# FFT filter and gated feed-forward on one core: the second and third transform stage as three products of high and low parts

## The chip, the core and the metric

The kernel runs on one NeuronCore of a Trainium2 chip. The metric is the time of one execution on the device in microseconds (us). A profile of one execution shows each engine's instructions: TensorE (PE, with its weight loads as PEld), VectorE (DVE), ScalarE (ACT), GpSimd (POOL) and SyncE (SP), which issues nearly all transfers.

## What is computed

```python
X = np.fft.rfft(x, axis=1)                      # x: 8 x 3136 x 256, float32
y = np.fft.irfft(X * (filt_r + 1j * filt_i), n=3136, axis=1)
h = np.maximum(y @ w_in, 0.0)                   # 256 -> 1024
conv = sum(conv_w[k] * shift(h, k - 1) for k in range(3))   # along the sequence
out = (h * sigmoid(conv)) @ w_out               # 1024 -> 256
```

The Fourier transform of length 3136 = 112 x 28 is done in four stages of small matrix products, two forward (kinds 1 and 2) and two back (kinds 3 and 4), with the filter between kinds 2 and 3.

## The kernel before

**Transform.** A batch has 14 pairs of columns; each kind works pair by pair, so a batch has 14 operations of each kind. Kind 1 multiplies input columns by tables `s1` that differ from column to column and stores to `a_dram`. Kind 2 (`second`, L233) reads `a_dram` in another order and multiplies by one constant matrix `s2` (112 x 120); the last pair uses `s2s` for its second half. `filt` (L240) multiplies by the filter: three multiplications on DVE (L244 to L246) from the PSUM bank and one addition on POOL (L247) that makes `z`. Kind 3 multiplies `z` by tables `i1`, which differ from column to column because they hold the frequency factors, and stores to `b_dram`. Kind 4 (`fourth`, L250) uses one constant matrix `m2`. All four are plain float32 products. The result y is kept in SBUF as a high part (rounded to the product type `F32R`, on ACT) and a low part (the rest, on DVE or POOL).

**Feed-forward.** The sequence of all batches is cut into units of 510 tokens; each unit has 8 slices of the hidden width. `inner` makes a slice's h in a PSUM bank with `mm3` (L174): three products, high x high, high x low, low x high, here twice for the two halves of the inner dimension. `relu`, `centre`, `sigmoid` and `round_g` run on ACT, `tap` (twice) and `gate` on DVE, `rest_g` (the low part of g, L150) on POOL. `project` adds the slice to two PSUM banks with twelve products of 256 columns; after a unit's eighth slice `evacuate` (L518) copies the two banks on DVE and stores them.

**Order.** Batch 0 goes through all four kinds at first by itself (about 118 us, loads, conversion of the weights from double precision, and no feed-forward). Then comes the main loop of single steps m, one slice each: 48 steps per batch. Every engine works through its own instructions in the order in which the loop emits them. In step m the transforms of later batches are issued ahead of `inner(m)`, and behind it `project` of the slice six steps earlier. The bank of a transform is read in the next step: `from_bank` stores kinds 1 and 3 (ACT copies, L226), runs `filt` for kind 2, and copies kind 4, whose parts `to_y` makes. `evacuate` stands ahead of `from_bank`. POOL's order in a step is: addition of `filt`, `rest_g` of the slice four steps back, then the low part of y.

**Plan.** Lists `at2` and `at4` say in which of the 48 steps kinds 2 and 4 of a batch are done; kind 3 follows three steps behind kind 2, and kind 1 of the next batch goes to the steps with the least work. From batch 2 on `at2 = [2 + 9*q//5 for q in range(14)]`: steps 2, 3, 5, 7, 9, 11, 12, 14, 16, 18, 20, 21, 23, 25. Batch 1 has its own list, and the last batch's span has no kind 1. Evacuations fall on steps 6, 14, 22, 30, 38 and 46.

**Buffers.** Transforms share two PSUM banks (`ps_t`), `inner` has four, `project` two. Inputs (`tin`) have five buffers and are loaded up to five operations ahead by `want_in`; tables (`tab`) have four, filters two, `z` three, `ot` three.

Of the kernel before, what the change touches and what calls it, by code (L numbers as in the profile page):

```python
# [19 lines left out]
G = 28  # L20
# [16 lines left out]
def _dft_tables():  # L37
# [6 lines left out]

    n1, n2, c, a = np.arange(N1), np.arange(N2), np.arange(N2), np.arange(N1)
    s1 = np.zeros((N1, N2, 112))
    m2 = np.zeros((112, N1))
    i1 = np.zeros((2, 2, 28, G, N2, 4))
    for g in range(G):
        for s in range(2):  # L50
            if g == G - 1 and s == 1:
                s1[:, :, 2 * 28 + g] = 1.0
                s1[:, :, 3 * 28 + g] = ((-1.0) ** n1)[:, None]
                m2[2 * 28 + g] = 1.0 / S
                m2[3 * 28 + g] = (-1.0) ** a / S
                i1[0, s, 0, g, :, 2] = 1.0
                i1[1, s, 0, g, :, 2] = (-1.0) ** c
                for j in range(14):
                    if j:
                        w = np.conj(_w(j * c, N2))  # L60
                        i1[0, s, j, g, :, 2] = 2 * w.real
                        i1[1, s, j, g, :, 2] = -2 * w.imag
                    w = np.conj(_w((56 + 112 * j) * c, S))
                    i1[0, s, 14 + j, g, :, 3] = 2 * w.real
                    i1[1, s, 14 + j, g, :, 3] = -2 * w.imag
# [5 lines left out]
            w = np.conj(_w(k1 * a, N1))  # L71
            m2[2 * s * 28 + g] = 2 * w.real / S
            m2[(2 * s + 1) * 28 + g] = -2 * w.imag / S
            for j in range(28):
                k2, sg = (j, 1) if j < 14 else (41 - j, -1)
                w = np.conj(_w((k1 + 112 * k2) * c, S))
                i1[0, s, j, g, :, 2 * s] = w.real
                i1[1, s, j, g, :, 2 * s] = -sg * w.imag
                i1[0, s, j, g, :, 2 * s + 1] = w.imag
                i1[1, s, j, g, :, 2 * s + 1] = sg * w.real  # L80

# [22 lines left out]

    i1 = i1.reshape(2, 56, G, 112)
    i1 = np.concatenate([i1[0], np.zeros((8, G, 112)), i1[1]])
    return {"s1": s1, "s2": s2(False), "s2s": s2(True), "one": np.eye(128), "i1": i1, "m2": m2}

# [14 lines left out]
def tile_fft_filter_gated_ffn(  # L123
# [11 lines left out]
    one: bass.AP,  # L135
    i1: bass.AP,
    m2: bass.AP,
    out: bass.AP,
):
# [48 lines left out]
    wc = ctx.enter_context(tc.tile_pool(name="wc", bufs=1))  # L188
    m2_sb = wc.tile([112, N1], F32, name="m2_sb")
    s2_sb = wc.tile([112, 120], F32, name="s2_sb")  # L190
    s2s_sb = wc.tile([112, 120], F32, name="s2s_sb")
    one_sb = wc.tile([128, 128], F32, name="one_sb")
    cw = wc.tile([128, 3, NF], F32, name="cw")
# [55 lines left out]

    def fourth(ps, br, m=m2_sb):  # L250
# [11 lines left out]
    with (  # L262
# [4 lines left out]
        raws, ws, fts, tabs, rows, zs, pss = {}, {}, {}, {}, {}, {}, {}  # L267
        m2g = sc.tile([112, N1], F32, name="m2g", bufs=1)
        bt = sc.tile([128, KT, G, 112], F32, name="bt", bufs=1)
# [66 lines left out]
        with tc.tile_pool(name="sq", bufs=2) as sq:  # L336
            at = sq.tile([128, KT, N2, 112], F32, name="at", bufs=1)

            def table(kind, c):
                k, src, n = {"1": (112, s1, 7), "3": (120, i1, 3)}[kind]  # L340
                tabs[kind, c] = t = sq.tile([120, 4, 112], F32, name=f"tab{kind}", bufs=n)[0:k]
                nc.sync.dma_start(out=t, in_=src[:, 4 * c:4 * c + 4])
# [11 lines left out]
            for c in range(7):  # L354
                table("1", c)
                load_x(0, 2 * c)
                load_x(0, 2 * c + 1)
                if c == 0:
                    load_conv()
                if c in (1, 3):  # L360
                    load_weights(c // 2)
                if c == 4:
                    for dst, src in ((one_sb, one), (s2_sb, s2[:, 0:120]), (s2s_sb, s2s[:, 0:120])):
                        nc.sync.dma_start(out=dst, in_=src)
# [15 lines left out]
            for i in range(NP + 4):  # L380
# [26 lines left out]
        for q in range(NP + 1):  # L407
# [3 lines left out]
            if q:  # L411
                ps = bank()
                fourth(ps, rows.pop(("4", q - 1)), m2g)
                yh, yl = y_slices(0, pair(q - 1))
# [103 lines left out]
    def evacuate(u, f):  # L518
        if f < NF - 1:
            return  # L520
        for k in range(2):
# [3 lines left out]
            n = part[0][1]  # L525
            ot = wp.tile([128, 2, D], F32, name="ot", bufs=3)
            nc.vector.tensor_copy(ot[0:n, 0:len(part)].rearrange("p t d -> p (t d)"), pos[u][k][0:n, 0:len(part) * D])  # L527
# [26 lines left out]
    for t in range(1, B):  # L554
        w = NW * (t - 1)
        used = [0] * NW
        if t == 1:
            at1 = [q // 2 for q in range(NP - AHEAD)]
            at2, at4 = [8 + 3 * q // 2 for q in range(NP)], [33 + 11 * q // NP for q in range(NP)]
            for q, s in enumerate(at1):  # L560
                put(s, "1", 1, AHEAD + q)
                used[s] += 1
        else:
            at2, at4 = [2 + 9 * q // 5 for q in range(NP)], [32 + 12 * q // NP for q in range(NP)]
        for q in range(NP):
            for s, kind, cost in ((at2[q], "2", 3), (at2[q] + 3, "3", 1), (at4[q], "4", 1)):
                put(w + s, kind, t, q)
                used[s] += cost
        if t + 1 < B:
# [5 lines left out]
            for q, s in enumerate(sorted(spots)):  # L575
                put(w + s, "1", t + 1, q)
        tails[w + 29] = heads[w + 45] = next(u for u in range(NU) if joins(u) and place(u)[0] == t - 1)
# [3 lines left out]
    tables = [op for _, op in order if op[0] in "13"]  # L581
    filters = [op for _, op in order if op[0] == "2"]
# [8 lines left out]
    def want_in():  # L591
        while wanted["in"] < min(done["in"] + 5, len(inputs)) and ready(inputs[wanted["in"]]):
            op = inputs[wanted["in"]]
            wanted["in"] += 1
            got_in[op] = load_in(tp, *op, 5, "tin")
# [13 lines left out]
    def transform(op):  # L609
        kind, b, q = op  # L610
        banks[op] = ps = ps_t.tile([128, 512], F32, name="ps_t")
        if kind in "124":
            done["in"] += 1
            r = got_in.pop(op)
        if kind in "13":
            want_table(done["table"] + 3)
# [35 lines left out]
    with tc.manual_schedule(engines=COMPUTE | {mybir.EngineType.SP}):  # L652
# [4 lines left out]
        for m in range(NF * NU + PLAG + 1):  # L657
# [78 lines left out]
```

## Time and profile before

| | |
|---|---|
| time, median of 3 runs | 1586.02 us (1585.51 to 1588.09) |
| profiled execution | 1583.21 us, its span 1581.2 us |
| mean granted TensorE clock | 0.991 |
| TensorE / DVE / ACT / POOL busy | 1532.2 / 1180.3 / 1150.4 / 821.7 us |
| instructions in the span | 26837 |

The span is the time from the first to the last instruction of the profiled execution. In a timeline row stand the start, the time taken, the engine, the line, the operation, what it writes and reads, its shapes and count, and in square brackets how long the engine had been idle and what ended that. A float32 product counts as two instructions on TensorE, one of high and low parts (`F32R`) as one. A matmul's recorded time contains its way through the array, so rows of successive matmuls overlap; the distance of starts tells how long one occupies TensorE. A row of a stretch shows its limits, its length, then busy time and number of instructions of PE, PEld, DVE, ACT and POOL, and at the end the granted TensorE clock, the share of the transfer engines and GB/s.

### The profile page before, as it was taken

How to read it: one execution, taken by the hardware profiler on the slowest of the kernel's cores; microseconds unless marked ns; L12 is line 12 of the kernel's file. 1: busy time of each engine (PE TensorE's matmuls, PEld its weight loads, DVE VectorE, ACT ScalarE, POOL GpSimd, SP SyncE). 2: the span in 40 equal slices, each digit the busy share in tenths (PEclk: the TensorE clock that was granted, in tenths of full speed). 3: DMA queues.
4: the chain of work that ended last, by engine and by line, in shares of the span. 5: the costliest groups of instructions: out<-in, count | busy, mean ns of one | idle time of the engine just before them, and what ended most of it. 6: DMA issues, size and time to landing. Idle time of an engine off the chain costs nothing.

```text
span 1581.2 us, 26837 instructions
## 1 busy us (share of the span) xinstructions
PE 1532.2 (97%) x9384; PEld 1334.5 (84%) x9384; DVE 1180.3 (75%) x1810; ACT 1150.4 (73%) x1989; POOL 821.7 (52%) x703
## 2 busy tenths in 40 slices
PE   6879999999999999999999999999999999999999
PEld 5777789878898889988898878987899878989998
DVE  5856876677767877777766787777866887777776
ACT  3367668866687668866688667876678666888886
POOL 2623455544575455744556454754457445664444
PEclk9989999999999999999999999999999999999999
DMA  9808764366634674277543766246742553300000
GB/s 271 261 24 246 226 192 140 119 204 178 186 88 143 201 218 125 74 209 210 155 139 107 212 179 184 85 148 198 211 135 63 179 155 106 96 14 28 27 28 30
DMA packets 160592, 229.16 MB, mean 145 GB/s; under 512 B 16546, under 2 KB 109578, under 8 KB 160458
## 3 DMA queue, kind: packets, MB, share of 16 engines
q1 hardware_dynamic: 159497, 226.53, 48.0%
q8 instruction: 75, 1.23, 0.3%
q10 hardware_dynamic: 960, 0.92, 0.2%
q14 instruction: 60, 0.48, 0.1%
HBM read 156.74 MB, written 70.65 MB: 144 GB/s over the span
## 4 chain that ended last, share of the span: by engine, by line
PE 87%; DMA 3%; issue 3%; ACT 2%; DVE 2%; POOL 1%; SPq 0%; ACTq 0%; POOLq 0%; DVEq 0%
PE ps_h L175 11%; PE ps_h L176 11%; PE ps_h L177 11%; PE po L514 11%; PE po L515 11%; PE po L516 11%; PE ps_t L231 10%; PE ps_t L255 6%; PE ps_t L235 5%; DMA rows<-in_x 1%; DMA f<-in_filt 1%; POOL g L150 1%; DMA tab<-in_i 1%; ACT y L144 0%; ACT br L327 0%
## 5 line engine op out<-in xcount | busy, mean ns | idle before, releaser
L482 DVE SCALAR_TENSOR_TENSOR t<-ps_h,cw,t 128x510 f32<-128x510 f32 (+1 forms) x800 | 588.3, 736 | 308.2 <-ACT t L478 305.0
L150 POOL TENSOR_TENSOR g<-t,g 128x510 fp32r<-128x510 f32 (+1 forms) x400 | 505.8, 1273 | 219.5 <-ACT g L144 203.9
L514 PE MATMUL po<-wo,g 128*128 128x256 f32 (+1 forms) x1576 | 439.3, 279 | 0.2 <-DVE ot L527 0.2
L515 PE MATMUL po<-wo,g 128*128 128x256 f32 (+1 forms) x1576 | 438.3, 278 | 0.0
L516 PE MATMUL po<-wo,g 128*128 128x256 f32 (+1 forms) x1576 | 438.0, 278 | 0.0
L473 ACT ACTIVATE ps_h<-ps_h 128x512 f32<-128x512 f32 (+1 forms) x400 | 234.7, 587 | 242.2 <-PE ps_h L177 240.7
L478 ACT ACTIVATE t<-ps_h,cw 128x510 f32<-128x510 f32 (+1 forms) x400 | 272.7, 682 | 103.4 <-POOL g L150 71.3
L247 POOL TENSOR_TENSOR z<-z,v 120x512 f32<-120x512 f32 x112 | 148.0, 1322 | 383.4 <-DVE v L246 314.6
L175 PE MATMUL ps_h<-y,wi 128*128 128x512 f32 (+1 forms) x688 | 325.3, 473 | 0.0
L514 PEld LDWEIGHTS po<-wo,g 128*128 128x128 f32 (+1 forms) x1576 | 296.6, 188 | 17.8 <-ACT t L478 0.6
L515 PEld LDWEIGHTS po<-wo,g 128*128 128x128 f32 (+1 forms) x1576 | 296.2, 188 | 16.6
L516 PEld LDWEIGHTS po<-wo,g 128*128 128x128 f32 (+1 forms) x1576 | 296.4, 188 | 0.6 <-POOL g L150 0.5
L176 PE MATMUL ps_h<-y,wi 128*128 128x512 f32 (+1 forms) x688 | 269.4, 392 | 0.2 <-DVE y L147 0.2
L488 DVE TENSOR_TENSOR t<-ps_h,t 128x510 f32<-128x510 f32 (+1 forms) x400 | 268.4, 671 | 0.9 <-ACT t L485 0.8
L177 PE MATMUL ps_h<-y,wi 128*128 128x512 f32 (+1 forms) x688 | 269.0, 391 | 0.0
L485 ACT ACTIVATE t<-t 128x510 f32<-128x510 f32 (+1 forms) x400 | 245.2, 613 | 1.8 <-DVE t L482 1.7
L144 ACT ACTIVATE g<-t 128x510 fp32r<-128x510 f32 (+1 forms) x400 | 245.1, 613 | 0.2 <-DVE t L488 0.2
L150 POOL TENSOR_TENSOR y<-z,y 128x448 fp32r<-128x448 f32 x98 | 138.7, 1425 | 97.4 <-ACT y L144 92.9
L175 PEld LDWEIGHTS ps_h<-y,wi 128*128 128x128 f32 x688 | 129.9, 189 | 35.9 <-issue 16.6
L176 PEld LDWEIGHTS ps_h<-y,wi 128*128 128x128 f32 x688 | 130.4, 190 | 34.4 <-issue 16.7
L177 PEld LDWEIGHTS ps_h<-y,wi 128*128 128x128 f32 x688 | 129.6, 188 | 29.8
L226 ACT ACTIVATE st<-ps_t 112x512 f32<-112x512 f32 x192 | 113.2, 591 | 10.9 <-PE ps_t L231 10.9
(81 smaller groups left out, 1657.9 us busy)
## 6 DMA issues: line engine op xcount, KB each, us to landing
filt<-in_filt SPq DMA_DIRECT2D x98, 512.0 KB
tin<-a_dram SPq DMA_DIRECT2D x98, 224.0 KB
b_dram<-st SPq DMA_DIRECT2D x98, 224.0 KB
tin<-b_dram SPq DMA_DIRECT2D x98, 224.0 KB
tin<-in_x SPq DMA_DIRECT2D x94, 224.0 KB
a_dram<-st SPq DMA_DIRECT2D x94, 224.0 KB
out<-ot SPq DMA_DIRECT2D x45, 256.0 KB
tab<-in_i SPq DMA_DIRECT2D x98, 105.0 KB
```

The lines of the kernel that those rows point to most:

```text
L144: nc.scalar.activation(dst, src, AF.Copy)
L150: nc.gpsimd.tensor_tensor(out=dst, in0=src, in1=hi.bitcast(F32), op=ALU.subtract)
L175: nc.tensor.matmul(ps, lhsT=wh, rhs=rh, start=start, stop=False, **kw)
L176: nc.tensor.matmul(ps, lhsT=wh, rhs=rl, start=False, stop=False, **kw)
L177: nc.tensor.matmul(ps, lhsT=wl, rhs=rh, start=False, stop=stop, **kw)
L478: nc.scalar.activation(t, hs[u, f][:, 1:n + 1], AF.Copy, scale=cw[:, 1, f:f + 1])
L482: nc.vector.scalar_tensor_tensor(out=t, in0=h[:, k:place(u)[2] + k], scalar=cw[:, k, f:f + 1], in1=t, op0=ALU.mult, op1=ALU.add)
L485: nc.scalar.activation(ts[u, f], ts[u, f], AF.Sigmoid)
L488: nc.vector.tensor_mul(ts[u, f], hs.pop((u, f))[:, 1:place(u)[2] + 1], ts[u, f])
L514: nc.tensor.matmul(o, lhsT=gh[:, c:c + n], rhs=wo[0][:, f], start=first, stop=False, skip_group_check=True)
L515: nc.tensor.matmul(o, lhsT=gh[:, c:c + n], rhs=wo[1][:, f], start=False, stop=False, skip_group_check=True)
L516: nc.tensor.matmul(o, lhsT=gl[:, c:c + n], rhs=wo[0][:, f], start=False, stop=last, skip_group_check=True)
```

## The change

Kinds 2 and 3 are done with `mm3`. Their constant matrices are split once, into `consts`, and their inputs are split for every operation in `split_in`: high part on ACT, low part on POOL, each at the end of that engine's work in the step. For a kind 2 of step m+1 this is done in step m, for a kind 3 of step m+2 also in step m. The factors that made kind 3's matrices differ move into kind 4's tables, so kind 3 has two constant matrices `s3` and `s3s`, and kind 4 has tables that differ from column to column: the per-operation tables are now loaded for kinds 1 and 4. Kind 3 stands four steps behind kind 2, not three; kind 4 starts one step later (two in batch 1). `tin` has four buffers and `ot` two. In batch 0 all products stay plain float32, with the constant `s3` turned once by POOL (`by_r`) and new tables for kind 4.

```diff
+    consts = {}
+    for name, t in (("s2", s2_sb), ("s2s", s2s_sb), ("s3", s3_sb), ("s3s", s3s_sb)):
+        consts[name] = [wp.tile(list(t.shape), F32R, name=f"{name}{h}", bufs=1) for h in range(2)]
+        hi_act(consts[name][0], t)
+        lo_pool(consts[name][1], t, consts[name][0])
...
-                nc.tensor.matmul(o, lhsT=br[:, j, 128 * k:128 * k + 128], rhs=m, start=True, stop=True)
+                nc.tensor.matmul(o, lhsT=br[:, j, 128 * k:128 * k + 128], rhs=tab[:, j], start=True, stop=True)
...
-            for c in range(2):
-                table("3", c)
             for q in range(3):
                 load_filter(q)
-            table("3", 2)
-            nc.sync.dma_start(out=m2_sb, in_=m2)
-            for r in range(4):
-                nc.sync.dma_start(out=m2g.rearrange("(g r) a -> r g a", r=4)[r], in_=m2[r * G:r * G + G])
+            for t, s in zip(by_r, (s3_sb, s3s_sb)):
+                nc.gpsimd.tensor_copy(t, s.rearrange("p (c r) -> p r c", r=4))
...
-                    ps = turned_stage(zs.pop(q), [tab("3", q)[:, j].rearrange("p (c r) -> p r c", r=4) for j in range(2)])
+                    ps = turned_stage(zs.pop(q), [by_r[q == NP - 1 and j].rearrange("p r c -> p (r c)") for j in range(2)])
                     nc.scalar.activation(bt[:, :, pair(q)], ps, AF.Copy)
-                    if q % 2 and q // 2 + 3 < 7:
-                        table("3", q // 2 + 3)
...
                 if i == 9:
                     for q in range(AHEAD):
                         load_x(1, q)
+                    for c in range(3):
+                        table("4", c)
...
-            ot = wp.tile([128, 2, D], F32, name="ot", bufs=3)
+            ot = wp.tile([128, 2, D], F32, name="ot", bufs=2)
...
-            at2, at4 = [2 + 9 * q // 5 for q in range(NP)], [32 + 12 * q // NP for q in range(NP)]
+            at2, at4 = [2 + 9 * q // 5 for q in range(NP)], [33 + 12 * q // NP for q in range(NP)]
         for q in range(NP):
-            for s, kind, cost in ((at2[q], "2", 3), (at2[q] + 3, "3", 1), (at4[q], "4", 1)):
+            for s, kind, cost in ((at2[q], "2", 3), (at2[q] + 4, "3", 1), (at4[q], "4", 1)):
...
-        while wanted["in"] < min(done["in"] + 5, len(inputs)) and ready(inputs[wanted["in"]]):
+        while wanted["in"] < min(done["in"] + 4, len(inputs)) and ready(inputs[wanted["in"]]):
...
-            k, src = {"1": (112, s1), "3": (120, i1)}[op[0]]
-            got_table[op] = t = tp.tile([120, 2, 112], F32, name="tab", bufs=4)[0:k]
+            src = {"1": s1, "4": m2}[op[0]]
+            got_table[op] = t = tp.tile([112, 2, 112], F32, name="tab", bufs=4)
...
-            second(ps, q, r)
-        if kind == "3":
-            by_column(ps, w, got_z.pop((b, q)))
+        if kind in "23":
+            rows_in, rows_out = {"2": (112, 120), "3": (120, 112)}[kind]
+            (rh, rl), o = parts.pop(op), ps[0:rows_out]
+            if q < NP - 1:
+                mm3(o, *consts[f"s{kind}"], *(t[0:rows_in].rearrange("p j d -> p (j d)") for t in (rh, rl)))
+            else:
+                for j, name in enumerate((f"s{kind}", f"s{kind}s")):
+                    mm3(o[:, j * D:j * D + D], *consts[name], rh[0:rows_in, j], rl[0:rows_in, j])
         if kind == "4":
-            fourth(ps, r)
+            fourth(ps, r, w)
+
+    def split_in(op):
+        kind, b, q = op
+        if kind == "2":
+            done["in"] += 1
+        r = got_in.pop(op) if kind == "2" else got_z.pop((b, q))
+        n = r.shape[0]
+        parts[op] = [wp.tile([128, 2, D], F32R, name=f"r{h}", bufs=3) for h in range(2)]
+        rh, rl = (t[0:n] for t in parts[op])
+        hi_act(rh, r)
+        return lambda: lo_pool(rl, r, rh)
...
             later = [to_y(op) for op in old]
+            later += [split_in(op) for k, kind in ((1, "2"), (2, "3")) for op in plan.get(m + k, []) if op[0] == kind]
             if p2:
                 gate(*p2)
             if p4:
                 rest_g(*p4)
             for step in later:
                 step()
```

More of the change, by code (lines that the diff above doesn't have):

```diff
@@ L55, in _dft_tables @@
                 m2[3 * 28 + g] = (-1.0) ** a / S
[L56 to L65, printed above, removed]
                 continue
@@ L70, in _dft_tables, with s3 @@
             s1[:, :, (2 * s + 1) * 28 + g] = w.imag
-            w = np.conj(_w(k1 * a, N1))
+            w = np.conj(_w(k1 * n, S))
             m2[2 * s * 28 + g] = 2 * w.real / S
             m2[(2 * s + 1) * 28 + g] = -2 * w.imag / S
+    def s3(special):
+        m = np.zeros((2, 2, 28, N2, 4))
+        for s in range(2):
             for j in range(28):
-                k2, sg = (j, 1) if j < 14 else (41 - j, -1)
[L76 to L80, printed above, removed]
+                if special and s == 1:
+                    if j == 0:
+                        m[0, s, 0, :, 2] = 1.0
+                        m[1, s, 0, :, 2] = (-1.0) ** c
+                    elif j < 14:
+                        w = np.conj(_w(j * c, N2))
+                        m[0, s, j, :, 2] = 2 * w.real
+                        m[1, s, j, :, 2] = -2 * w.imag
+                    else:
+                        w = np.conj(_w((56 + 112 * (j - 14)) * c, S))
+                        m[0, s, j, :, 3] = 2 * w.real
+                        m[1, s, j, :, 3] = -2 * w.imag
+                    continue
+                k2, sg = (j, 1) if j < 14 else (41 - j, -1)
+                w = np.conj(_w(k2 * c, N2))
+                m[0, s, j, :, 2 * s] = w.real
+                m[1, s, j, :, 2 * s] = -sg * w.imag
+                m[0, s, j, :, 2 * s + 1] = w.imag
+                m[1, s, j, :, 2 * s + 1] = sg * w.real
+        m = m.reshape(2, 56, 112)
+        return np.concatenate([m[0], np.zeros((8, 112)), m[1]])
     def s2(special):
@@ L103, in s2 @@
         return np.concatenate([re, gap, im, -im, gap, re], 1)
-    i1 = i1.reshape(2, 56, G, 112)
-    i1 = np.concatenate([i1[0], np.zeros((8, G, 112)), i1[1]])
-    return {"s1": s1, "s2": s2(False), "s2s": s2(True), "one": np.eye(128), "i1": i1, "m2": m2}
+    turned = m2.reshape(4, G, N2, N1).transpose(1, 0, 2, 3).reshape(112, N2, N1)
+    return {"s1": s1, "s2": s2(False), "s2s": s2(True), "one": np.eye(128), "s3": s3(False), "s3s": s3(True), "m2": m2, "m2g": turned}
 def _bins():
@@ L135, in tile_fft_filter_gated_ffn @@
     one: bass.AP,
-    i1: bass.AP,
+    s3: bass.AP,
+    s3s: bass.AP,
     m2: bass.AP,
+    m2g: bass.AP,
     out: bass.AP,
@@ L248, in filt, with fourth @@
         return z
-    def fourth(ps, br, m=m2_sb):
+    def fourth(ps, br, tab):
         for j in range(2):
@@ L267, in tile_fft_filter_gated_ffn @@
         raws, ws, fts, tabs, rows, zs, pss = {}, {}, {}, {}, {}, {}, {}
-        m2g = sc.tile([112, N1], F32, name="m2g", bufs=1)
+        by_r = [sc.tile([120, 4, N2], F32, name=f"by_r{i}", bufs=1) for i in range(2)]
         bt = sc.tile([128, KT, G, 112], F32, name="bt", bufs=1)
@@ L339, in table @@
             def table(kind, c):
-                k, src, n = {"1": (112, s1, 7), "3": (120, i1, 3)}[kind]
-                tabs[kind, c] = t = sq.tile([120, 4, 112], F32, name=f"tab{kind}", bufs=n)[0:k]
+                pool, src, n = {"1": (sq, s1, 7), "4": (sc, m2g, 3)}[kind]
+                tabs[kind, c] = t = pool.tile([112, 4, 112], F32, name=f"tab{kind}", bufs=n)
                 nc.sync.dma_start(out=t, in_=src[:, 4 * c:4 * c + 4])
@@ L362, in tile_fft_filter_gated_ffn @@
                 if c == 4:
-                    for dst, src in ((one_sb, one), (s2_sb, s2[:, 0:120]), (s2s_sb, s2s[:, 0:120])):
+                    for dst, src in ((one_sb, one), (s2_sb, s2[:, 0:120]), (s2s_sb, s2s[:, 0:120]), (s3_sb, s3), (s3s_sb, s3s)):
                         nc.sync.dma_start(out=dst, in_=src)
@@ L412, in tile_fft_filter_gated_ffn @@
                 ps = bank()
-                fourth(ps, rows.pop(("4", q - 1)), m2g)
+                fourth(ps, rows.pop(("4", q - 1)), tab("4", q - 1))
+                if q % 2 == 0 and q // 2 + 2 < 7:
+                    table("4", q // 2 + 2)
                 yh, yl = y_slices(0, pair(q - 1))
@@ L558, in tile_fft_filter_gated_ffn @@
             at1 = [q // 2 for q in range(NP - AHEAD)]
-            at2, at4 = [8 + 3 * q // 2 for q in range(NP)], [33 + 11 * q // NP for q in range(NP)]
+            at2, at4 = [8 + 3 * q // 2 for q in range(NP)], [35 + 10 * q // NP for q in range(NP)]
             for q, s in enumerate(at1):
@@ L576, in tile_fft_filter_gated_ffn @@
                 put(w + s, "1", t + 1, q)
-        tails[w + 29] = heads[w + 45] = next(u for u in range(NU) if joins(u) and place(u)[0] == t - 1)
+        tails[w + 29] = heads[w + 46] = next(u for u in range(NU) if joins(u) and place(u)[0] == t - 1)
         assert NF * tails[w + 29] >= w + NW
@@ L580, in tile_fft_filter_gated_ffn @@
     inputs = [op for _, op in order if op[0] in "124"]
-    tables = [op for _, op in order if op[0] in "13"]
+    tables = [op for _, op in order if op[0] in "14"]
     filters = [op for _, op in order if op[0] == "2"]
@@ L611, in transform @@
         banks[op] = ps = ps_t.tile([128, 512], F32, name="ps_t")
-        if kind in "124":
+        if kind in "14":
             done["in"] += 1
             r = got_in.pop(op)
-        if kind in "13":
             want_table(done["table"] + 3)
```

13 lines of the change are left out of this document (8 added, 5 removed).

## The prediction

> **What bounds the kernel now.** I read the page's busy shares, the chain, the stretches by window, then the timeline of one transform stage.
>
> ```profile
> PE 1532.2 (97%) x9384; PEld 1334.5 (84%) x9384; DVE 1180.3 (75%) x1810; ACT 1150.4 (73%) x1989; POOL 821.7 (52%) x703
> ...
> PE 87%; DMA 3%; issue 3%; ACT 2%; DVE 2%; POOL 1%; SPq 0%; ACTq 0%; POOLq 0%; DVEq 0%
> ...
> 668.00:768.00 100.00, 98.54 (x563) 82.15 (x563) 79.47 (x120) 68.48 (x122) 45.72 (x37) 1.00 0.65 192
> ```
>
> TensorE has 97% of the span and 87% of the chain. In the third row (columns PE, PEld, DVE, ACT, POOL) it stays at 98.5% through the second and third stage of one batch, while POOL is under half busy. So TensorE work removed there should shorten the time, if POOL and ACT deliver its operands in time. A loop step m is: transforms, `inner`, `project`. I number the 48 steps of a batch 0 to 47, and call the transform kinds 1 to 4.
>
> **TensorE's saving.**
>
> ```profile
> 670.62 0.40 PE L175 MATMUL ps_h<-y,wi 128*128 128x512 f32 x1
> ...
> 673.43 0.40 PE L175 MATMUL ps_h<-y,wi 128*128 128x512 f32 x1
> ...
> 740.89 1.02 PE L235 MATMUL ps_t<-tin,s_sb 112*120 112x512 f32 x2
> ...
> 744.55 1.03 PE L231 MATMUL ps_t<-z,tab 120*112 120x256 f32 x4
> ...
> 705.80 0.40 PE L177 MATMUL ps_h<-yx,wi 128*128 128x512 f32 x1
> ...
> 706.03 0.40 PE L175 MATMUL ps_h<-yx,wi 128*128 128x512 f32 x1
> ```
>
> A step without a transform takes 673.43-670.62 = 2.81 us; one with a kind 2 takes 744.55-740.89 = 3.66, so the operation costs 0.85. Kind 3 is four passes of the same columns and gets the same 0.85. Products of high and low parts are those of L175 to L177, which start 0.23 apart at 512 columns: three cost 0.69. The last pair's six products of 256 columns stream the same columns. Saving 0.16 x 196 operations (7 batches x 28) = 31.4 us. Bounds: 0.15 and 0.17, 29 to 33.
>
> **ACT.** 196 new high parts of 112 or 120 x 512, nearest rows g L144 and st L226, at about 0.6.
>
> ```profile
> L144 ACT ACTIVATE g<-t x400: 276/619/631, 128.7 to 1576.9; 128x510 fp32r<-128x510 f32 x131, 128x105 fp32r<-128x105 f32 x3
> ...
> L150 POOL TENSOR_TENSOR g<-t,g x400: 411/1291/1352, 129.4 to 1577.2; 128x510 fp32r<-128x510 f32 x131, 128x105 fp32r<-128x105 f32 x3
> ```
>
> About one per step: 0.6 of 3.7. With ACT 68% busy in the stage (31.5 idle of 100 us) that fits between its waits; cost 0. If the cover went, relu and the taps behind it would be late.
>
> **POOL, the term that decides.** 196 low parts at 1.29 (second row) are 253 us. By share they fit (821.7+253 of 1581, 68%). But POOL works in order. In step s its queue is z (L247, which waits for the filter's last multiplication on DVE), rest_g (L150), and now behind them the low part of the kind 2 of step s+1, for which TensorE waits in its second product. So where a kind 2 stands at s-1 and another at s+1, the second waits for filter + z + g + low part of the first. Kind 3 is split two steps ahead and has a step of slack. The plan for t>=2 puts kind 2 at steps 2,3,5,7,9,11,12,14,16,18,20,21,23,25. The worst place is step 22, where `evacuate` stands ahead of the filter on DVE:
>
> ```profile
> 763.96 1.40 DVE L527 COPY ot<-po 128x512 f32<-128x512 f32 x2 [1.33 <-PE po L516]
> ...
> 764.47 1.03 PE L231 MATMUL ps_t<-tin,tab 112*112 112x256 f32 x4
> ...
> 765.27 0.68 DVE L244 TENSOR_TENSOR z<-ps_t,filt 120x512 f32<-120x512 f32 x1
> ...
> 766.66 0.69 DVE L246 SCALAR_TENSOR_TENSOR v<-ps_t,filt 56x512 f32<-56x512 f32 x1
> ...
> 767.44 1.28 POOL L247 TENSOR_TENSOR z<-z,v 120x512 f32<-120x512 f32 x1 [4.24 <-DVE v L246]
> ...
> 768.68 2.52 POOL L150 TENSOR_TENSOR g<-t,g 128x510 fp32r<-128x510 f32 x2
> ```
>
> Step 22 begins at 764.47. The copies wait for the end of step 21's `project`, so all of this hangs on the step's own start. The first of the two g ends at 769.94; a low part behind it ends at 771.23, 6.76 after the step's start. The new plan leaves only a kind 3 in step 22 (0.69+2.81 = 3.50), then the first product of the kind 2 of step 23 (0.23): TensorE waits 3.0 us. So it is in batches 2 to 7; in batch 1 a kind 1 fills 0.87 of it: 6 x 3.0 + 2.2 = 20.2 us.
>
> Three more places in each batch, from the same rows of other steps (and the wait of a kind 1 in step 6, which stays):
>
> ```profile
> 687.19 1.02 PE L235 MATMUL ps_t<-tin,s_sb 112*120 112x512 f32 x2
> ...
> 693.12 2.53 POOL L150 TENSOR_TENSOR g<-t,g 128x510 fp32r<-128x510 f32 x2
> ...
> 695.36 1.02 PE L235 MATMUL ps_t<-tin,s_sb 112*120 112x512 f32 x2
> ...
> 700.75 1.12 PE L231 MATMUL ps_t<-tin,tab 112*112 112x256 f32 x4 [0.72 <-ACT st L226]
> ...
> 703.22 2.54 POOL L150 TENSOR_TENSOR g<-t,g 128x510 fp32r<-128x510 f32 x2
> ...
> 725.60 1.02 PE L235 MATMUL ps_t<-tin,s_sb 112*120 112x512 f32 x2
> ...
> 730.72 2.54 POOL L150 TENSOR_TENSOR g<-t,g 128x510 fp32r<-128x510 f32 x2
> ...
> 760.69 1.09 PE L235 MATMUL ps_t<-tin,s_sb 112*120 112x512 f32 x2 [0.50 <-PE ps_t L231]
> ```
>
> From the start of a kind 2 to the end of a low part behind the first g (+1.27+1.29) it is 8.5 us (step 3), 10.4 (step 5) and 7.7 (step 12). TensorE has 7.4, 9.5 and 7.2 of work up to the second product of the next kind 2 (3 to 5: 0.69+2.81+0.85+2.81+0.23). Waits 1.1, 0.9 and 0.5 in a batch; in batch 7, without kind 1, the first two are 2.0 and 2.5; batch 1 has one like the first. 5 x 2.0 + 4.5 + 1.1 + 6 x 0.5 = 18.6. A wait lets DVE catch up, which brings the next filter forward, so I take half, 9, and keep 0 and 18.6. The 0.50 in the last row, at step 21, goes, since there a kind 3 stands between the two kind 2: -0.5 x 6 = -3. Waits together +26 (17 to 36).
>
> **The granted clock** (third column from the right) fell to half in the first 100 us where TensorE idled, always at the end of a stretch of 3.41 us:
>
> ```profile
> 8.01:11.42 3.41, 1.93 (x17) 1.75 (x16) 0.95 (x3) 1.63 (x3) 0.00 (x0) 1.00 1.06 280
> ...
> 35.31:38.73 3.42, 1.71 (x7) 0.62 (x5) 3.30 (x5) 0.85 (x2) 2.44 (x3) 1.00 1.02 362
> ...
> 72.86:76.27 3.41, 1.79 (x9) 1.42 (x8) 3.31 (x6) 1.15 (x3) 1.68 (x1) 1.00 1.05 294
> ...
> 76.27:79.69 3.42, 2.72 (x12) 2.33 (x11) 3.26 (x6) 0.54 (x1) 3.38 (x3) 0.50 0.13 43
> ...
> 42.14:45.55 3.41, 3.41 (x14) 2.88 (x15) 3.31 (x6) 1.11 (x2) 1.51 (x1) 0.50 0.85 256
> ...
> 45.55:48.97 3.42, 3.42 (x17) 2.67 (x16) 2.80 (x5) 1.12 (x3) 1.78 (x1) 1.00 0.83 290
> ...
> 93.34:96.75 3.41, 3.27 (x15) 3.27 (x16) 0.17 (x1) 1.76 (x4) 0.95 (x6) 0.50 0.07 23
> ...
> 96.75:100.17 3.42, 3.42 (x18) 3.42 (x17) 2.88 (x5) 1.78 (x3) 0.00 (x0) 0.50 0.00 0
> ```
>
> It fell after a stretch with 1.79 busy, not after 1.93 (nor after one of 1.71), and came back after a full one. A wait of 3.0 us leaves more than 1.6 idle in one of two neighbouring stretches in nine placings of ten. The price is half of one or two stretches at half rate, 1.7 or 3.4 us: 2.4 at each of the seven waits, +16.8 (0 to 24). The Trainium skill, "TensorE: Matmul & The Clock Gate", section "What's actually happening", has the clock fall only after at least one whole idle window of about 3.4 us. By that rule a wait of 3.0 costs no clock and the sum ends at 1578.6; the row with 1.79 busy disagrees with it.
>
> **The first 118 us.**
>
> ```profile
> 33.76 8.43 DMA tab<-in_i
> ...
> 62.69 8.43 DMA f<-in_filt
> ...
> tab<-in_i SPq DMA_DIRECT2D x7, 210.0 KB
> ...
> tab<-in_s SPq DMA_DIRECT2D x7, 196.0 KB
> ```
>
> Up to 79 us transfers pace this part (two of its longest chain pieces). Seven tables of 210 KB go: 1.5 MB at 280 GB/s (row 8.01) is 5.3 us. Three of the seven new ones, each as large as a kind 1's (196 KB), are queued on SP ahead of the last filters: 2.1 back; the other four load after 79 us, where the transfers are idle. -3 (0, if DVE paces it, to -6). The five small loads of `m2` go and two of `s3` come; the two turned copies run on POOL while it waits; reading `by_r` in order saves TensorE time that DVE's filters cover. The eight splits of the constants stand ahead of the first steps on ACT and POOL: at most four ACT operations of 0.6, at least nothing: +1.
>
> **At no cost.** 98 tables for kind 4 in place of 98 for kind 3. Four `tin` buffers, not five, and kind 2's freed by POOL: SP waits longer at such a load, with tables and filters queued behind it; the lead is still four operations, over 10 us. If that cover went, filters would be late on DVE. Two `ot` buffers serve one unit, eight steps apart. Kind 3 and 4 a step later keep their distances.
>
> **Sum** against the profiled execution (1583.2; span 1581.2): -31.4 + 26 + 16.8 - 3 + 1 = +9.4, 1592.6. The median shown, 1586.0, is 2.8 higher: 1595.4.
>
> **Rivals.**
> B, the clock stays up: the stretch with 1.71 busy speaks for it, that of 1.79 against. 1595.4 - 16.8 = 1578.6, or 1568 to 1589 with the ends of the waits. This is where the page's rule ends too.
> C, the low parts are in time: DVE and ACT get so far ahead of a shorter TensorE stage that z is not late. It decides if step 22's low part ends 3.7 us after the step begins, not 6.8. POOL's 54 idle us of 100 speak for it; the copies that wait for `project` ahead of the filter speak against. With a third of the waits, 9, and full clock: 1586.0 - 31.4 + 9 - 3 + 1 = 1561.6 (1552 to 1571).
> D, the products don't run at 0.23 with 112 or 120 rows: at the recorded 0.39 each they cost 1.17, +0.32 x 196 instead of the saving, above 1640. The starts 0.23 apart speak against; 2 in 100.
>
> **How the numbers follow.** Forecast (waits and clock) 0.55, its own range 1582 to 1608; B 0.25; C 0.18; D 0.02. No change means within 0.2%, 1582.8 to 1589.2, about what a measurement tells. The forecast falls 0.06 faster, 0.12 same, 0.37 slower; B 0.17, 0.05, 0.03; C 0.18 faster; D slower: 0.41, 0.17, 0.42. The range 1562 to 1608 leaves out half of C, D and the forecast's upper end.
>
> **What would show it.** Second products waiting for POOL's low part, longest (3 us) once in each batch, in the step after an evacuation with a filter; a granted clock of 0.5 for 3 to 7 us behind each; steps with one kind 2 or 3 at 3.50 us elsewhere; POOL near 1075 us busy, ACT near 1250. It would be wrong if those waits were under 1.5 us, if the clock stayed at 1.0 behind them, or if a group of three products took more than 0.75.

## The result and the profile after

The changed kernel takes 1609.55 us (median; 1607.65 to 1610.37), the kernel before on the same chip 1585.76 us: 1.015 of the time before, 95% interval 1.0129 to 1.0171. The direction and the mechanism were those of the forecast; the time is 14 us above the predicted value and 1.5 us above the upper end of the range.

The page of the changed kernel, busy times; then the first row of its view of waits (who waited, for whom, us in total, times, longest):

```profile
PE 1520.0 (95%) x9412; PEld 1344.0 (84%) x9412; DVE 1181.0 (73%) x1810; ACT 1252.2 (78%) x2189; POOL 1071.9 (67%) x905
```

```profile
PE ps_t L186 <- POOL r L160: 31.6, 20, 2.9
```

ACT and POOL are as busy as forecast (1250 and 1075). The wait is new: 20 times, 31.6 us in all and up to 2.9 us at once, TensorE stood at the second product of a kind 2 (L186) for the low part `r`. Here is the longest kind, at step 23 of batch 3, from the timelines of TensorE, DVE and POOL of the changed kernel:

```profile
591.35 0.40 PE L185 MATMUL ps_t<-r,s 112*120 112x512 f32 x1
594.61 0.50 PE L186 MATMUL ps_t<-r,s 112*120 112x512 f32 x1 [2.86 <-POOL r L160]
```

```profile
587.35 1.40 DVE L541 COPY ot<-po 128x512 f32<-128x512 f32 x2 [0.82 <-PE po L530]
588.66 0.68 DVE L255 TENSOR_TENSOR z<-ps_t,filt 120x512 f32<-120x512 f32 x1
589.35 0.68 DVE L256 TENSOR_TENSOR v<-ps_t,filt 56x512 f32<-56x512 f32 x1
590.05 0.69 DVE L257 SCALAR_TENSOR_TENSOR v<-ps_t,filt 56x512 f32<-56x512 f32 x1
```

```profile
590.82 1.28 POOL L258 TENSOR_TENSOR z<-z,v 120x512 f32<-120x512 f32 x1 [3.76 <-DVE v L257]
592.06 1.26 POOL L160 TENSOR_TENSOR g<-t,g 128x510 fp32r<-128x510 f32 x1
593.28 1.28 POOL L160 TENSOR_TENSOR r<-tin,r 112x512 fp32r<-112x512 f32 x1
```

Read them from below: the low part at 593.28 needed neither of the two operations ahead of it in POOL's queue. POOL had been idle 3.76 us, because the addition of `z` at the head of the queue waited for the filter, and the filter stood behind the evacuation on DVE. Where there is no wait, a step with one kind 2 or 3 is as short as forecast, 3.49 us:

```profile
552.92 0.40 PE L185 MATMUL ps_t<-r,s 120*112 120x512 f32 x1
...
556.41 0.39 PE L185 MATMUL ps_t<-r,s 112*120 112x512 f32 x1
```

The waits cost clock too. Stretches of the changed kernel (busy time of PE first; the clock is third from the right), first around the wait that ends at 594.61, then around the like wait (2.86 us) in batch 2, which ends at 408.36:

```profile
591.48:594.90 3.42, 0.56 (x3) 0.28 (x2) 2.12 (x5) 1.54 (x3) 3.42 (x4) 1.00 0.22 68
594.90:598.31 3.41, 3.41 (x10) 2.69 (x9) 3.15 (x5) 0.87 (x3) 3.41 (x4) 0.51 0.68 195
403.74:407.16 3.42, 1.76 (x14) 1.43 (x12) 2.75 (x5) 1.10 (x4) 2.58 (x3) 1.00 0.47 144
407.16:410.57 3.41, 2.21 (x11) 1.86 (x12) 2.72 (x5) 2.26 (x5) 3.41 (x3) 1.00 0.38 100
```

The first wait lies in one stretch and the next runs at half clock; the second is divided over two and costs none. The main loop has eight such drops, 13.7 us of lost clock, where the kernel before has none. Six follow waits for the low part; two, in batch 1, follow waits of a kind 1 (3.07 and 1.89 us).

Two things had not been forecast. In the profiled executions the first feed-forward product starts later, not earlier (kernel before, then changed):

```profile
118.37 0.59 PE L175 MATMUL ps_h<-y,wi 128*128 128x512 f32 x1
```

```profile
120.91 0.58 PE L185 MATMUL ps_h<-y,wi 128*128 128x512 f32 x1
```

And the products of `project`, which the change does not touch, run slower. First and last of the twelve of one step, before and after:

```profile
1001.14 0.28 PE L514 MATMUL po<-wo,g 128*128 128x256 f32 x1
...
1002.41 0.28 PE L516 MATMUL po<-wo,g 128*128 128x256 f32 x1
```

```profile
1013.65 0.28 PE L528 MATMUL po<-wo,g 128*128 128x256 f32 x1
...
1014.95 0.28 PE L530 MATMUL po<-wo,g 128*128 128x256 f32 x1
```

Eleven distances take 1.27 us before and 1.30 after. Over some 4300 distances of each timeline (steps at half clock left out) the mean is 115.3 and 117.5 ns. In the last 90 us, where no transform is left, it is 114.5 and 117.4, so the transforms beside it are not the cause. With 4728 products, 2.2 ns each are 10.4 us.

### The profile page after: what moved, and what is told of

Its sections match the earlier page's. It is cut to its first block, busy times and chain, and to the rows that moved or that the text cites. A ratio compares the mean times of both kernels' runs of the same rounds, so it can differ in the third digit from the quotient of the medians.

```text
span 1607.7 us, 27205 instructions
## 1 busy us (share of the span) xinstructions
PE 1520.0 (95%) x9412; PEld 1344.0 (84%) x9412; DVE 1181.0 (73%) x1810; ACT 1252.2 (78%) x2189; POOL 1071.9 (67%) x905
## 5 line engine op out<-in xcount | busy, mean ns | idle before, releaser
L185 PE MATMUL ps_h<-y,wi 128*128 128x512 f32 (+1 forms) x688 | 291.1, 423 | 0.0
L187 PE MATMUL ps_h<-y,wi 128*128 128x512 f32 (+1 forms) x688 | 271.8, 395 | 0.0
L186 PE MATMUL ps_h<-y,wi 128*128 128x512 f32 (+1 forms) x688 | 271.7, 395 | 0.0
L186 PEld LDWEIGHTS ps_h<-y,wi 128*128 128x128 f32 x688 | 131.3, 191 | 21.1
L160 POOL TENSOR_TENSOR r<-tin,r 112x512 fp32r<-112x512 f32 x98 | 127.3, 1299 | 30.8 <-ACT r L154 26.8
```

Of the source, the lines that this page charges most:

```text
L160: nc.gpsimd.tensor_tensor(out=dst, in0=src, in1=hi.bitcast(F32), op=ALU.subtract)
L185: nc.tensor.matmul(ps, lhsT=wh, rhs=rh, start=start, stop=False, **kw)
L186: nc.tensor.matmul(ps, lhsT=wh, rhs=rl, start=False, stop=False, **kw)
L187: nc.tensor.matmul(ps, lhsT=wl, rhs=rh, start=False, stop=stop, **kw)
```

## The experiments

In what follows, "waits of the main loop" are all idle times of TensorE over 0.15 us behind the first feed-forward product, summed from its timeline (before 17.6 us, changed 47.1), and "lost clock" is one minus the granted clock, summed over the main loop without its last 10 us. All ratios are to the kernel before on the same chip. Runs that build on each other are told in their order.

**The order of POOL's queue.** The addition of `filt` is returned instead of issued, and issued behind the low part of the next kind 2:

```diff
-        nc.gpsimd.tensor_tensor(out=z, in0=z, in1=v, op=ALU.add)
-        return z
+        return z, lambda: nc.gpsimd.tensor_tensor(out=z, in0=z, in1=v, op=ALU.add)
...
-            later += [split_in(op) for k, kind in ((1, "2"), (2, "3")) for op in plan.get(m + k, []) if op[0] == kind]
+            later += [split_in(op) for op in plan.get(m + 1, []) if op[0] == "2"]
+            later += adds
+            adds = []
+            later += [split_in(op) for op in plan.get(m + 2, []) if op[0] == "3"]
```

> The changed kernel with one instruction of POOL's queue moved: the addition of z, which waits for DVE's filter, stands behind the low part of the next second product instead of ahead of it; no instruction is added or taken away. Theory 'queue order': the waits of TensorE for POOL's low part (2.9 us at step 23 of each batch, those of steps 5 and 14, and batch 7's) go, about -28 us, and with them most of the 14.0 us at the lower clock, about -10; so about 1571 (1566 to 1578), TensorE waiting under 20 us in the main loop instead of 48. Rival 'POOL's load' (the low part is late because POOL has too much to do, in whatever order): waits and time stay, about 1609. The spacing of the projection's products stays at 0.1176 in either case.

Measured: 1564.79 us, ratio 0.9873 (0.9853 to 0.9893): faster than the kernel before, and a little below the expected range. The same place of batch 3 on POOL and TensorE in this kernel:

```profile
577.60 1.29 POOL L160 TENSOR_TENSOR g<-t,g 128x510 fp32r<-128x510 f32 x1
580.17 1.30 POOL L160 TENSOR_TENSOR r<-tin,r 112x512 fp32r<-112x512 f32 x1 [1.28 <-ACT r L154]
581.42 1.30 POOL L258 TENSOR_TENSOR z<-z,v 120x512 f32<-120x512 f32 x1
```

```profile
581.89 0.40 PE L185 MATMUL ps_t<-r,s 112*120 112x512 f32 x1
582.12 0.40 PE L186 MATMUL ps_t<-r,s 112*120 112x512 f32 x1
```

The low part is now done at 581.47, before its kind 2 begins, and no L186 waits over 0.15 us anywhere. Waits fall from 47.1 to 16.3 us, lost clock from 13.7 to 1.7. These two make 43 of the 46.0 us between the profiled executions (1609.44 and 1563.44). POOL does as much as before (1070.8 us busy), so its load was not the cause. "Queue order" is shown.

**The third stage alone.** Kind 2 goes back to `second` in plain float32, and only kind 3 is split:

```diff
-        if kind in "23":
+            done["in"] += 1
+            second(ps, q, got_in.pop(op))
+        if kind == "3":
...
-            later += [split_in(op) for k, kind in ((1, "2"), (2, "3")) for op in plan.get(m + k, []) if op[0] == kind]
+            later += [split_in(op) for k, kind in ((2, "3"),) for op in plan.get(m + k, []) if op[0] == kind]
```

> The changed kernel with the second stage back in plain float32: only the third stage is done as three products. Half of the saving on TensorE goes (98 operations times 0.16, +15.7), and with it every wait for the low part of a second product. Theory 'the waits are those of the second stage's low part': TensorE's waits in the main loop fall from 48 us to about 18, its clock drops nearly vanish (-12), so 1609.5 + 15.7 - 30 - 12 = about 1583. Rival 'waits come from POOL's added work in general': half of it is left, so half of the waits and drops: about 1604.

Measured: 1576.51 us, 0.994 (0.9925 to 0.9955), 6 us under the expected time; waits 14.8 us, lost clock 1.7. The waits came with the split of the second stage; half of POOL's added work, that for the third, makes none. Since waits and clock are nearly those of the run above, the two give the price of an operation: the profiled executions are 12.8 us apart, the first feed-forward product starts 2.0 us earlier here and the waits are 1.4 less, so 98 kinds 2 in float32 cost 16.2 us more, 0.165 each. The 0.16 of the prediction holds for kind 2; kind 3 was not measured by itself.

**Work in the wait.** Twelve copies of the first product fill the wait of step 23 in batches 2 to 7:

```diff
+            if kind == "2" and b > 1 and q == 12:
+                for _ in range(12):
+                    nc.tensor.matmul(o, lhsT=consts["s2"][0], rhs=rh[0:rows_in].rearrange("p j d -> p (j d)"), start=True, stop=True)
```

> The changed kernel with twelve further copies of the first product (512 columns, 0.23 us each, 2.8 us together, overwritten by the product that follows) ahead of the second stage's three products in step 23 of batches 2 to 7, where TensorE waits 2.9 us for POOL. The wait is filled with work and not shortened. Theory 'idle time lowers the clock': the drops to half behind step 23 (four of eight in the profile of the changed kernel, 1.7 us each) go, about -7 us, so about 1602. Rival 'the drops have another cause': the time stays within 2 us of 1609.5. If TensorE's wait is not fixed by POOL, the copies would add up to 6 x 2.8 = 17 us.

Measured: 1602.38 us, 1.0106 (1.0087 to 1.0125), some 7 us less than the changed kernel although TensorE has 17 us more to do. The same stretches in this kernel:

```profile
591.48:594.90 3.42, 3.41 (x17) 2.41 (x15) 2.08 (x4) 1.15 (x3) 3.42 (x3) 1.00 0.22 67
594.90:598.31 3.41, 3.28 (x20) 2.94 (x21) 3.38 (x6) 2.13 (x5) 3.41 (x4) 1.00 0.60 153
```

The clock stays up behind step 23 in all six batches. Lost clock falls from 13.7 to 1.7 us; the start loses 3.4 us more (18.8 against 15.4). Only four of the seven drops that are gone stood at step 23. The waits in front of the other three are still there (2.0 us in batch 1, 1.7 and 2.2 in batch 7), so these went by the chance of where the stretches fall, and the price of a single drop can't be read from this time. Where the wait is filled, though, no drop follows: idle time does lower the clock, and its price is real time: doing useless work there is faster than standing still.

**The place of the operands.** The addresses in SBUF had changed with the buffers: by 512 bytes, the weights `wi` and `wo` stand at remainder 96 before and 32 after, the high part of g at 160 and 224. The low part is 256 bytes further, every slice a multiple of 512. The kernel before, with padding only:

```diff
+    wc.tile([128, 112], F32, name="pad_c")
     wi = [wc.tile([128, KT, FF], F32R, name=f"wi{h}") for h in range(2)]
...
+    wp.tile([128, 32], F32, name="pad_w", bufs=1)
     ring = [[wp.tile([128, UO + 66], F32R, name=f"g{i}{h}", bufs=1) for h in range(2)] for i in range(4)]
```

> This is the kernel before, instruction for instruction, with 448 bytes of padding ahead of the weights and 128 ahead of the ring of g, so that wi, wo, y, g and t stand at the remainders by 512 bytes that they have in the changed kernel (wi and wo 32 instead of 96, g 224 and 480 instead of 160 and 416). Theory 'placement': the 256-column products of the projection start 0.1176 us apart instead of 0.1154, which over some 4800 of them is +10.6 us, so about 1596. Rival 'not placement' (something that the changed kernel does beside these products): they stay 0.1154 apart and the time stays at 1586 within 3.

Measured: 1594.1 us, 1.0053 (1.0035 to 1.0072), spacing 117.3 ns. Padding alone makes the kernel before slower, and its `project` nearly as slow as in the changed one. Next, the two operands moved one at a time, and both to multiples of 64 (the same two pads, of 448 and 64, 0 and 64, 416 and 448 bytes):

> The kernel before with 448 bytes of padding ahead of the weights and 64 ahead of the ring: wi and wo at remainder 32 (as in the changed kernel), g at 160 and 416 (as before). Theory 'the moving operand's place': spacing 0.1173 as with both moved, about 1594. Rival 'the stationary operand's place': 0.1153, about 1586. A third, 'only the distance of the two matters': neither.

> The kernel before with 64 bytes of padding ahead of the ring alone: g at 224 and 480 (as in the changed kernel), wi and wo at 96 (as before). The counterpart of the run with the weights moved. Theory 'the moving operand's place (the weights)': 0.1153, about 1586. Rival 'the stationary operand's place': 0.1173, about 1594.

> The kernel before with 416 bytes of padding ahead of the weights and 448 ahead of the ring: wi, wo and g at remainder 0 by 64 bytes (by 512: 0, and 0 and 256). If the spacing of the projection's products comes from operands that straddle a boundary of 64 bytes, it falls below 0.1153 us (towards the 0.107 that the 512-column products' 0.232 would give by half... 0.116 by half of 0.232, so little), and the time goes below 1583. If only the place by 512 matters, it is anywhere between 0.115 and 0.118: 1584 to 1596.

Measured: 1601.6 us, 1.0103 (1.0084 to 1.0122); 1600.02, 1.0093 (1.0068 to 1.0119); 1602.49, 1.0101 (1.0075 to 1.0128). Neither operand by itself and no boundary of 64 bytes: moving either is worse than moving both, and full alignment has the longest spacing (119.2 ns). The first and last product of a step in the kernel with the weights moved:

```profile
1003.72 0.28 PE L516 MATMUL po<-wo,g 128*128 128x256 f32 x1
...
1005.03 0.28 PE L518 MATMUL po<-wo,g 128*128 128x256 f32 x1
```

That is 1.31 us for eleven distances. What orders all runs is the third theory, the distance of g from `wo`; two more distances were tried on the kernel below, which has 64 again (32 bytes more ahead of the ring; 480 more, with narrower `t`):

> The kernel with the queue order and the placement changed, and g 32 bytes further: its distance from wo is 96 by 256 bytes. So far distances 64, 192, 128 and 0 by 256 gave 0.1153, 0.1175, 0.1189 and 0.1192 us from one product of the projection to the next. If the spacing is a smooth function of the distance with its least value at 64, 96 gives 0.116 to 0.117, +3 to +8 us: 1564 to 1569. If its least value lies between 64 and 192, 96 gives 0.1153 or less: 1561 or below.

> The counterpart, with g at a distance of 32 by 256 bytes from wo (480 bytes of padding ahead of the ring, and t 512 instead of 576 columns wide to make room for it). Smooth with the least value at 64: 0.116 to 0.1175, 1564 to 1571. If the least value lies below 64: 0.1153 or less, 1561 or below.

They gave 1568.79 us, 0.9896 (0.9872 to 0.9919), and 1567.27, 0.9887 (0.9865 to 0.9909), against 1560.82 with distance 64. Their spacing, 118.2 ns, is longer than either theory said, so the least value is a narrow one. 3.0 ns more for 4728 products would be 14 us, and the time rose by 6 to 8: the granted clock averaged 0.988 in these executions and 0.983 in those with distance 64, and 0.005 of 1560 is 8 us the other way.

| distance of g from wo, by 256 bytes | spacing of `project`, ns | kernels |
|---|---|---|
| 0 | 119.2 | all aligned |
| 32 | 118.2 | distance 32 |
| 64 | 115.3, 115.2, 115.1 | before; queue and placement; changed, placed as before |
| 96 | 118.2 | distance 96 |
| 128 | 118.9, 118.8 | weights moved; ring moved |
| 192 | 117.5, 117.3 | changed; before, placed as after |

The kernel before happened to have the best of the six distances tried. That the distance alone counts rests on 128, which two different pairs of places give with the same spacing; the other distances were each tried with one pair of places.

**Placement in the changed kernel.** With its late low parts left alone, only the placement of before (64 bytes ahead of the weights, the ring allocated ahead of `consts`):

> The changed kernel with its queue order left alone and only the placement of the kernel before (64 bytes of padding ahead of the weights, the ring of g ahead of the high and low constants). Theory 'placement': spacing 0.1153 instead of 0.1175, 4800 x 0.0022 = -10.6, so about 1599, which was the upper end of 1608 less; the waits for POOL's low part stay at 2.9 us at step 23. What the clock makes of those waits can move by some drops of 1.7 us, since their place in time moves: 1594 to 1604. Rival 'the spacing in the changed kernel is not from the placement': 1609.

Measured: 1602.68 us (1598.0 to 1609.07), 1.0108 (1.0083 to 1.0133); spacing 115.1 ns, so the theory holds for the changed kernel. In its profiled execution, however, the first feed-forward product starts 2.2 us later than in the changed kernel and the waits are 51.1 us, 4.0 more, so not all of the 11 us is seen in the median. The executions of this kernel lie 11 us apart; the profiled one is the fastest, with 5.1 us of lost clock.

With the queue order too:

> The kernel with z behind the low parts, and beside it the weights, y and g back at the remainders by 512 bytes that they have in the kernel before (wi and wo 96, g 160 and 416; 64 bytes of padding ahead of the weights, and the ring of g allocated ahead of the high and low constants). Theory 'placement': the projection's products return from 0.1175 to 0.1153 us apart, 4800 x 0.0021 = -10 us, so about 1555 (1552 to 1558). Rival 'the spacing follows something else in the changed kernel, and the placement only matters in the kernel before': 0.1175 and 1565 again.

Measured: 1560.82 us, 0.9849 (0.983 to 0.9867), 4 us less and not 10. Spacing is 115.2 ns as expected; the profile shows where the rest went: 8.5 us of lost clock instead of 1.7, and 18.8 instead of 17.1 in the first 118 us. All four executions bear it out: their granted clock averages 0.9828, against 0.9873 with the queue order alone, and 0.0045 of 1560 is 7 us. A kind 1 at step 6 waits 1.73 to 1.75 us here, and 1.58 to 1.60 with the queue order alone; here two of these waits were followed by a drop, there none; two more drops are in batch 1.

**The loads at the start.** The two constants of `s3` behind the third load of weights, the three tables of kind 4 behind the last filter:

```diff
-                    for dst, src in ((one_sb, one), (s2_sb, s2[:, 0:120]), (s2s_sb, s2s[:, 0:120]), (s3_sb, s3), (s3s_sb, s3s)):
+                    for dst, src in ((one_sb, one), (s2_sb, s2[:, 0:120]), (s2s_sb, s2s[:, 0:120])):
...
             load_weights(2)
+            for dst, src in ((s3_sb, s3), (s3s_sb, s3s)):
+                nc.sync.dma_start(out=dst, in_=src)
...
-                    for c in range(3):
-                        table("4", c)
+                if i == 12:
+                    for c in range(3):
+                        table("4", c)
```

> The kernel with the queue order and the placement changed, and beside it two sets of loads of the first stretch moved: the two constants of the third stage behind the third load of weights, and the three tables of the first batch's fourth stage behind the last filter instead of ahead of the filters of columns 22 to 27. Theory 'the queue of loads delays the first batch': DVE waits less than 1 us for that filter instead of 4.8, the first feed-forward product starts at 118.4 as in the kernel before instead of 121.7, so about -3: 1558. Rival 'the filters come late anyway' (the kernel before, too, waits there for x rows and for POOL): within 1 us of 1561.

Measured: 1557.61 us, 0.9825 (0.9804 to 0.9846). DVE's wait for the filter, in the changed kernel and in this one:

```profile
72.58 0.69 DVE L255 TENSOR_TENSOR z<-ps,f 120x512 f32<-120x512 f32 x1 [3.40 <-DMA f<-in_filt]
```

```profile
70.63 0.69 DVE L256 TENSOR_TENSOR z<-ps,f 120x512 f32<-120x512 f32 x1 [2.19 <-DMA f<-in_filt]
```

With queue and placement alone that wait was 4.81 us. The first feed-forward product starts at 118.75, 3.0 us earlier, as expected; the wait did not fall under 1 us. In the whole time the gain (3.2 us) is inside the intervals, and one profiled execution does not show it either, because this start scatters. The first product comes at 117.4 to 121.1 us in the five kernels that load as the kernel before does (it and the four with padding alone), at 119.1 to 123.1 in the eight that load as the changed one does, and at 118.75 and 116.94 in the two with the loads moved. So the order of the loads probably costs 2 to 3 us. That this filter is the reason is not shown: the four kernels with padding alone wait for it 2.4 to 3.0 us too.

This kernel's profiled execution has 12.0 us of lost clock, though all of its regular waits are short. Here is one that cost clock and one that did not (batches 2 and 4):

```profile
335.16:338.57 3.41, 1.65 (x8) 1.02 (x8) 3.35 (x6) 2.20 (x6) 3.41 (x4) 1.00 0.75 241
338.57:341.98 3.41, 3.41 (x13) 2.95 (x12) 1.11 (x2) 1.54 (x3) 2.18 (x2) 0.50 0.72 212
696.97:700.38 3.41, 1.90 (x14) 1.39 (x12) 2.83 (x5) 2.99 (x6) 3.41 (x4) 1.00 0.76 265
700.38:703.80 3.42, 3.19 (x18) 2.79 (x19) 2.52 (x4) 1.36 (x3) 3.42 (x3) 1.00 0.63 185
```

The waits are of 1.76 and 1.74 us. The first falls into one stretch, which keeps 1.65 us of work, and the next runs at half clock; the second is cut by a limit. Whether these cost what they seem to was the last question. The kind 1 that waits was moved:

```diff
-                s = min(range(5 if t == 1 else 0, NW - 2), key=lambda s: (used[s], s))
+                s = min((s for s in range(5 if t == 1 else 0, NW - 2) if t == 1 or s - 4 not in at2), key=lambda s: (used[s], s))
```

> The kernel with queue order, placement and order of loads changed, and in batches 2 to 6 the one first-stage product pair that shares step 6 with a third-stage product moved to step 34 (none stands any more in a step with a third-stage product). In step 6 TensorE waited 1.75 us in each of these batches, and in the profile of that kernel the clock fell behind four of these five waits. Theory 'a wait of 1.75 us costs its own length and, where it falls badly against the 3.41 us stretches, a further 1.7 us at half clock': the waits go (5 x 1.75 = 8.7 us) and with them the drops (8.5 us in that profile, about half of it on the average of placements), so 1557.6 - 8.7 - 4 = about 1545 (1541 to 1550), and the executions of the kernel lie closer together than the 7 us of before. Rival 'the wait moves': the pair waits in step 34 behind the evacuations of the fourth stage for as long: 1557.

Measured: 1542.18 us, 0.9726 (0.971 to 0.9743), executions from 1540.7 to 1543.9 instead of 1555.3 to 1562.3. From the waits of TensorE, first the kernel with the loads moved, then this one:

```profile
PE ps_t L243 <- ACT st L238: 10.7, 6, 1.9
```

```profile
PE ps_t L243 <- ACT st L238: 2.5, 2, 1.9
```

Waits of the main loop fall from 19.0 to 10.4 us and lost clock from 12.0 to 1.7 (four of the six drops that are gone stood behind the moved kind 1; two were in batch 1, which the edit leaves as it was). Of the 15.4 us between the medians 8.6 are the waits, 1.8 the start (first product at 116.94), and about 5 are left for the clock, averaged over executions whose limits fall differently. Their granted clocks, 0.985 and 0.988 on average, agree: 0.003 of 1550 is 5 us. This is the fastest version: 2.7% under the kernel before, with all of the change in it.

## Why the prediction was wrong in size and right in kind

Point by point:

- **TensorE's saving, -31.4.** Held: steps of 3.49 us, and 0.165 per kind 2 from the run with the third stage alone.
- **Waits for POOL's low part, +26.** The chain evacuate, filter, z, g, low part is the one in the trace. Step 23 waited 2.83 to 2.89 us (3.0 forecast), step 5 1.0 (1.1), step 14 0.7 (0.5), batch 7 1.7 and 2.2 (2.0 and 2.5); step 7 did not wait in batches 2 to 6, and the 2.2 us of batch 1 did not come. The wait of a kind 1 at step 6, which was to stay at 0.72, became 1.38. In all the main loop waits 29.5 us more than before. Too low by 3.5: the step that halved the smaller places had no row behind it; without the halving the term would have been 35.8, and the truth lies between.
- **Clock, +16.8.** 13.7: eight drops of 1.7 us each. The estimate of 2.4 per drop was too high (never two stretches). "Nine placings in ten" was not met, since two of the six waits at step 23 cost none, but six are few. Four drops were not forecast, at waits of 1.7 to 3.1 us in batches 1 and 7; that the total came close is in part luck. By the rule of the Trainium skill ("TensorE: Matmul & The Clock Gate", section "What's actually happening") the clock falls after a whole idle window. The trace disagrees: it fell behind stretches that still held 0.56 us of work (changed kernel) and 1.65 us (kernel with the loads moved).
- **The first 118 us, -3, and the constants, +1.** Not met: +2.5 in the profiled executions. The step took the tables' transfer time as a sum of bytes. The order of the loads is the likelier cause, but single executions scatter by 4 us here, and the way by which the order acts stays open.
- **"At no cost", and the sum.** This is the step that failed. The changed buffers were put at nothing after a look at their lead times alone, and the sum had no term for work that the change leaves as it is. But the buffers move addresses: `project`'s products take 2.2 ns more each, +10.4 us, the largest miss. A run with padding alone and one with the old placement show that it is the placement. Start +4.5, waits +3.5, clock -3.1 and `project` +10.4 against the forecast's terms make 15.3 of the 16.8 us by which 1592.6 missed the profiled 1609.44; the clock term's excess hid some of the miss.

Rival B (clock stays up) is refuted by the lost clock of 13.7 us and by the run with work in the wait. Rival C (low parts in time) did not happen. Its 1561.6 is close to what the kernel gives (1564.79) when one instruction changes its place in POOL's queue, but by luck: C still had 9 us of waits, which are gone there, and it lacked the 10.4 us of `project`.

## What to carry to other kernels

When work is added to an engine that has time to spare, look at its queue, not its share: an instruction that waits holds up what stands behind it, and here one place in the order was worth some 45 us. Short waits of the bounding engine cost more than their length where they lower its clock, so a regular wait of 1.7 us is worth removing. Any change of buffers moves all addresses behind them: compare the spacing of products that the change doesn't touch, before looking for a cause in the change.

## What the runs showed of the hardware

- The spacing of `project`'s products (256 columns, new weights for each) depends on where the two operands lie to each other: 115.2 to 119.2 ns, by the distance of the stationary from the moving operand modulo 256 bytes, with the least at 64 of the six distances tried. That is up to 3.5% of such a product. The Trainium skill ("TensorE: Matmul & The Clock Gate", section "Step-by-step: what each phase is for") states that two read ports let the next weights load without taking read bandwidth from the running product. The table above does not fit that without something added; that the two reads meet in the memory would explain it, and no run here shows it. Other distances, and what this does for 512 columns (232.3 ns before, 232.6 to 233.1 in the others), stay open.
- The clock fell behind stretches of 3.41 us in which TensorE had work for less than about half, but the limit is not sharp. With the stretches cut where the clock of the same execution changes, one with 1.58 us of work stayed up in the kernel before; in the changed kernel one with 1.70 (the first stretch of the like wait above) stayed up, and one with 1.71 was followed by half clock:

```profile
1274.35:1277.76 3.41, 1.58 (x5) 1.03 (x6) 3.35 (x6) 1.47 (x3) 1.64 (x2) 1.00 0.28 29
1277.76:1281.18 3.42, 3.42 (x22) 3.04 (x22) 3.36 (x6) 2.31 (x4) 1.91 (x2) 1.00 0.74 258
```

```profile
403.80:407.21 3.41, 1.70 (x14) 1.37 (x12) 2.69 (x4) 1.09 (x4) 2.63 (x3) 1.00 0.47 144
407.21:410.62 3.41, 2.26 (x11) 1.92 (x12) 2.77 (x5) 2.26 (x5) 3.41 (x3) 1.00 0.39 105
1263.98:1267.39 3.41, 1.71 (x9) 1.18 (x8) 2.07 (x4) 2.37 (x5) 3.41 (x4) 1.00 0.07 11
1267.39:1270.80 3.41, 3.41 (x14) 3.09 (x13) 0.81 (x2) 1.77 (x3) 2.45 (x2) 0.50 0.57 210
```

Work as the trace models it is therefore not an exact measure.

- Batch 0's third stage reads its moving operand in steps of four elements in the kernel before, and in order (`by_r`) in the changed one. Eight of its products take 1.78 and 1.04 us at full clock (first row of each pair, before and changed), and 2.05 in both at half clock (second row):

```profile
54.73 1.78 PE L317 MATMUL ps<-tab,z 120*128 120x112 f32 x8
82.42 2.05 PE L317 MATMUL ps<-tab,z 120*128 120x112 f32 x8 [2.59 <-POOL z L247]
```

```profile
54.73 1.04 PE L328 MATMUL ps<-by_r,z 120*128 120x112 f32 x8
83.78 2.05 PE L328 MATMUL ps<-by_r,z 120*128 120x112 f32 x8 [2.59 <-POOL z L258]
```
